# Window attention with a positional convolution: later LayerNorm statistics, value copies on VectorE, an earlier convolution start and edge loads on two queues

## The chip, the cores and the metric

The kernel runs on one core of a Trainium2 chip. Times are device microseconds (us) of one execution. A run of a kernel gives one time, and a kernel is run several times in rounds that alternate with the kernel before on the same chip. Engines in the profile: PE is TensorE (PEld its weight loads), DVE is VectorE, ACT is ScalarE, POOL is GpSimd, SP is SyncE, which here only issues transfers.

## The reference, cut

```python
# x: (1, 511, 511, 192) bf16, dw_pe: (3, 3, 192), w_qkv: (192, 576), w_o: (192, 192)
x0 = x + depthwise_conv3x3(x, dw_pe)              # positional encoding
h  = layernorm(x0)                                # over the 192 channels, no weights
hw = windows(h, 7)                                # 73 x 73 windows of 49 tokens
q, k, v = split_heads(hw @ w_qkv, heads=4)        # head dimension 48
out = softmax(q @ k.T * 48 ** -0.5) @ v           # inside each window
return x0 + unwindow(out @ w_o)
```

## The kernel before: the parts that matter

The 5,329 windows are cut into 42 blocks (0 to 41) of up to 128 windows, one window to a partition. A block goes through attention in 16 chunks of 8 windows. Three blocks are under way at any time:

- block b is in attention (stages A for q, E, A for k, V, the output projection of the block before, D, B);
- block b+1 has its convolution in chunks 0 to 6, its LayerNorm statistics in chunks 6 to 12 and its transposes in chunks 8 to 14;
- block b+2 is loaded: XP (the padded image for the convolution) once XP is free, then X (the windows). The first 30 of its 192 convolution matmuls are done in chunk 15 ("early").

PSUM has three two-bank slots named `ps` for attention, and two slots named `psc`, which the convolution and the LayerNorm transposes share. Blocks 36 to 40 hold vertical strips of the image's edge, and block 41 nine short strips that need many small loads. Since block b+2 is loaded during block b, this shows in blocks 34 to 39, which are called the edge blocks below.

```python
def conv_mm(cv):                       # one convolution matmul; after ten, one addition on VectorE
    c = cv.c
    if c % 10 == 0:
        cv.ps = PCB.next()             # psc
    mm(cv.ps[:, (c % 10) * S : (c % 10 + 1) * S], lhsT=XP[0:KP, :, c], rhs=T[0:KP, c, :], start=True, stop=True)
    cv.c += 1
    if cv.c % 10 == 0 or cv.c == C:
        ...                            # the addition needs X, which is loaded after XP
        nc.vector.tensor_tensor(out=xv, in0=cv.ps[...], in1=xv, op=ALU.add)

def ln_tr(b, r, h):                    # one row of LayerNorm transposes: both psc slots, then two copies
    pb = []
    for kt in range(2):
        pb.append(PCB.next()[0:KT, :].bitcast(BF))
        ...                            # 7 transposes on TensorE
    for kt in range(2):
        eng = nc.vector.tensor_copy if kt == 0 else nc.scalar.copy
        eng(out=HO[b % 2][...], in_=pb[kt][...])
...
# main loop, chunk g = (b, ck); f0 and f are its start and end as a fraction of the block
conv_goal = (EARLY if b else 0) + part(0.0, 0.39, C - (EARLY if b else 0))      # EARLY = 30
if n and conv.c == C and n.tr == WS and nn and xpn == len(xp) and xln == len(xl):
    conv, conv_goal = nn.conv, part(0.875, 1.0, EARLY)      # only when all transposes are done
...
def fill(weight):                      # convolution matmuls between those of stages A and V
    quota[0] += (conv_goal - conv_start) * weight / 24
    ...
s_goal = part(0.40, 0.76, len(n.items)) if n else 0         # statistics
...                                    # hook(share): statistics, stores and loads that are due
stage_A(b, ck, 0, fill)                # q
hook(0.15)
stage_E(*groups[g - LE], nc.vector.tensor_copy)
stage_A(b, ck, 1, fill)                # k
hook(0.35)
stage_V(b, ck, fill, nc.scalar.copy, vv[g % 2])
...                                    # rest of the chunk's convolution
hook(0.55)
...                                    # projection of block b-1: proj(b - 1, s0), copied by ScalarE to pO
stage_D(vv[(g - LD) % 2])
stage_B()
hook(0.75)
n.transpose(part(0.51, 0.88, WS), 1.0)                      # LayerNorm transposes, one row a call
hook(1.0)
```

## Time and profile before

| | before |
|---|---|
| median time | 3900.07 us (3888.94 to 3900.96, 3 runs) |
| profiled execution | 3887.3 us |
| mean of blocks 1 to 33 | 87.61 us |
| block 39 (loads of block 41) | 143.8 us |
| time at half clock, mean of blocks 1 to 33 | 0.4 us a block |

A block's length is the distance between the q copies of its first chunk and of the next block's; chunk lengths are read in the same way. The time at half clock is computed from the mean granted clock c of a block of length t: 2(1 - c)t, because the records show full and half clock only.

The prediction shows the main lines. Two more of the waits of the kernel before are needed later. Each line is an engine, its tile and line, what it waited for, then the sum in us, the number of waits and the longest.

```profile
PE psc L315 <- DVE HO L358: 27.9, 28, 1.0
...
PE psc L348 <- POOL h L338: 14.7, 37, 0.5
```

The first is the early convolution waiting for the copy of the last transposes to give a psc slot free: 1.0 us at most. The second is a row of transposes waiting for its normalized row from GpSimd. Both are small. Line numbers move by up to three lines between the kernels; the tile names identify the group.

### The profile page before, as it was taken

How to read it: one execution, taken by the hardware profiler on the slowest of the kernel's cores; microseconds unless marked ns; L12 is line 12 of the kernel's file. 1: busy time of each engine (PE TensorE's matmuls, PEld its weight loads, DVE VectorE, ACT ScalarE, POOL GpSimd, SP SyncE). 2: the span in 40 equal slices, each digit the busy share in tenths (PEclk: the TensorE clock that was granted, in tenths of full speed). 3: DMA queues.
4: the chain of work that ended last, by engine and by line, in shares of the span. 5: the costliest groups of instructions: out<-in, count | busy, mean ns of one | idle time of the engine just before them, and what ended most of it. 6: DMA issues, size and time to landing. Idle time of an engine off the chain costs nothing.

```text
span 3887.3 us, 165790 instructions
## 1 busy us (share of the span) xinstructions
PE 3422.5 (88%) x75049; PEld 3029.4 (78%) x75049; DVE 2519.8 (65%) x4238; ACT 2799.0 (72%) x3508; POOL 2049.4 (53%) x1427
## 2 busy tenths in 40 slices
PE   3999999999999999999999999999999988888587
PEld 3788888888888888888888888888888877777476
DVE  6666666666666666666666666666666666666453
ACT  0677777777777777777777777777777777666465
POOL 4255555555555555555555555565555555555443
PEclk9799999999999999999999999999999999999888
DMA  5233344444433344444433344444433333344221
GB/s 135 68 93 93 93 100 106 111 112 110 112 94 93 93 100 101 109 114 110 116 94 93 93 101 100 110 112 111 111 100 94 93 93 93 93 93 93 55 40 43
DMA packets 529108, 377.12 MB, mean 97 GB/s; under 512 B 453595, under 2 KB 453787, under 8 KB 528393
## 3 DMA queue, kind: packets, MB, share of 16 engines
q1 hardware_dynamic: 527927, 366.14, 38.9%
q8 instruction: 589, 9.65, 1.1%
q14 instruction: 126, 1.03, 0.1%
q10 hardware_dynamic: 466, 0.30, 0.0%
HBM read 265.31 MB, written 100.27 MB: 94 GB/s over the span
## 4 chain that ended last, share of the span: by engine, by line
PE 31%; DVE 13%; ACT 7%; DMA 4%; SPq 3%; issue 2%; POOL 1%; ACTq 0%; POOLq 0%; DVEq 0%
PE ps L370 10%; PE psc L315 6%; ACT pO L476 5%; PE ps L386 5%; DVE bnst L326 4%; PE ps L465 4%; PE ps L453 4%; DMA X<-in_x_dram 4%; DVE HO L358 3%; DVE o L439 3%; ACT v L394 2%; SPq L238 2%; PE ps L429 2%; DVE HO L454 1%; DVE rs L438 1%
## 5 line engine op out<-in xcount | busy, mean ns | idle before, releaser
L480 POOL TENSOR_TENSOR X<-X,pO 128x768 bf16<-128x768 bf16 (+1 forms) x539 | 831.9, 1562 | 1610.9 <-ACT pO L476 1610.9
L370 PE MATMUL ps<-HO,Wqk 96*128 96x392 bf16 x5336 | 1379.3, 338 | 90.0 <-ACT pO L476 69.7
L315 PEld LDWEIGHTS <-XP 81*128 81x128 bf16 x8064 | 1108.6, 176 | 195.3 <-issue 100.7
L315 PE MATMUL psc<-T,XP 81*128 81x49 bf16 x8064 | 1061.1, 217 | 140.7 <-DMA XP<-in_x_dram 40.3
L321 DVE TENSOR_TENSOR X<-psc,X 128x490 bf16<-128x490 f32 x840 | 541.9, 645 | 436.9 <-PE psc L315 315.4
L378 ACT CAST k<-ps 128x784 bf16<-128x784 f32 x667 | 542.1, 813 | 377.5 <-PE ps L370 304.5
L378 ACT CAST q<-ps 128x784 bf16<-128x784 f32 x667 | 542.8, 814 | 272.5 <-PE ps L370 266.4
L338 POOL TENSOR_TENSOR h<-X,rstd 128x1344 bf16<-128x1344 bf16 x287 | 697.8, 2431 | 22.5
L370 PEld LDWEIGHTS <-Wqk 96*128 96x128 bf16 x5336 | 565.6, 112 | 153.6 <-issue 38.9
L386 PE MATMUL ps<-Wv,HO 96*128 96x192 bf16 x5336 | 643.5, 247 | 26.7 <-ACT q L378 20.1
L416 ACT ACTIVATE pt<-ps 128x784 bf16<-128x784 f32 x667 | 550.3, 825 | 156.8 <-PE ps L408 141.5
L439 DVE TENSOR_TENSOR o<-ps,rs 128x768 bf16<-128x768 f32 x667 | 638.4, 957 | 23.2
L386 PEld LDWEIGHTS <-HO 96*128 96x128 bf16 x5336 | 522.7, 105 | 143.3 <-issue 106.3
L394 ACT CAST v<-ps 128x768 bf16<-128x768 f32 x667 | 536.6, 805 | 117.7 <-PE ps L386 113.5
L438 DVE RECIPROCAL rs<-ps 128x16 f32<-128x16 f32 x667 | 171.3, 257 | 692.6 <-PE ps L429 545.2
L326 DVE BATCH_NORM_STATS2 bnst<-X 128x6 f32<-128x384 bf16 x1050 | 519.5, 543 | 3.0
L454 DVE COPY HO<-ps 96x784 bf16<-96x784 bf16 x667 | 377.2, 566 | 164.2 <-PE ps L453 160.3
L336 POOL TENSOR_TENSOR rstd<-rstd,expo 128x7 f32<-128x7 f32 x294 | 435.4, 1481 | 24.5
L453 PEld LDWEIGHTS <-o 128*96 128x96 bf16 x5336 | 377.3, 128 | 76.5 <-DVE o L439 39.7
L465 PE MATMUL ps<-Wo,HO 96*128 96x192 bf16 x4116 | 435.7, 258 | 0.7 <-DVE HO L454 0.7
L453 PE MATMUL ps<-ident,o 128*96 128x128 bf16 x5336 | 425.2, 223 | 4.5 <-DVE o L439 3.1
L476 ACT CAST pO<-ps 128x768 bf16<-128x768 f32 x498 | 387.3, 801 | 40.9 <-PE ps L465 25.2
(55 smaller groups left out, 2886.7 us busy)
## 6 DMA issues: line engine op xcount, KB each, us to landing
XP<-in_x_dram SPq DMA_DIRECT2D x648, 216.0 KB
X<-in_x_dram SPq DMA_DIRECT2D x574, 168.0 KB
out_dram<-X SPq DMA_DIRECT2D x246, 336.0 KB
XP<-in_x_dram SPq DMA_DIRECT2D x71, 212.6 KB
out_dram<-X SPq DMA_DIRECT2D x82, 168.0 KB
XP<-in_x_dram SPq DMA_DIRECT2D x16, 192.0 KB
XP<-in_x_dram SPq DMA_DIRECT2D x56, 30.4 KB
X<-in_x_dram SPq DMA_DIRECT2D x9, 165.4 KB
```

The source lines that it names most:

```text
L315: mm(cv.ps[:, (c % 10) * S : (c % 10 + 1) * S], lhsT=XP[0:KP, :, c], rhs=T[0:KP, c, :], start=True, stop=True)
L326: nc.vector.bn_stats(out=bnst[:, s : s + 2, :].rearrange("p a f -> p (a f)"), in_=self.X[b % 3][:, s : s + 2, :].rearrange("p s c -> p c s"),)
L338: eng.tensor_tensor(out=h[:, :, :], in0=self.X[b % 3][:, t, :], in1=rstd[:, t].unsqueeze(2).to_broadcast([128, WS, C]), op=ALU.mult)
L370: mm(ps[:, ab * 512 : ab * 512 + TOK], lhsT=self.Wqk[kt][0:KT, which * 2 + ab, :], rhs=HO[b % 2][0:KT, kt, ck * CH : (ck + 1) * CH, 0:S], ...
L378: nc.scalar.copy(out=dst[:, :, 0:TOK], in_=two_bank(ps, TOK))
L386: mm(ps[:, col : col + C], lhsT=HO[b % 2][0:KT, kt, w : w + 2, :].rearrange("p w s -> p (w s)"), rhs=self.Wv[kt][0:KT, :], start=(kt == 0) ...
L394: eng(out=v_[:].rearrange("p (b j) h e -> p b (j h) e", b=2)[:, :, :, 0:DH], in_=two_bank(ps, 2 * C).rearrange("p b (g d) -> p b g d", d=DH),)
L439: nc.vector.tensor_tensor(out=o_[:].rearrange("p b q (h d) -> p b (q h) d", d=DH), in0=ov[:, :, :, 0:DH], in1=r_[:].rearrange("p (b g) -> ...
L453: mm(ev, lhsT=o_[:, sl, Q, kt * KT : (kt + 1) * KT], rhs=ident[:], start=True, stop=True, is_transpose=True)
L465: mm(ps[:, col : col + C], lhsT=HO[b % 2][0:KT, kt, :, s0 + i], rhs=self.Wo[kt][0:KT, :], start=(kt == 0), stop=(kt == 1))
L476: nc.scalar.copy(out=o[:].rearrange("p (b s) c -> p b (s c)", b=2), in_=two_bank(ps, 2 * C))
L480: nc.gpsimd.tensor_tensor(out=xv, in0=xv, in1=o[:, 0:n, :], op=ALU.add)
```

## The change

The intent is to spread VectorE's work: statistics and transposes run up to the end of the block, and VectorE copies v where it has no statistics. Convolution of the block after next starts in chunk 14, before the last transposes. The small loads of block 41, the only one with more than two strips, are issued on two queues. The core of the diff:

```diff
+    q = nc.scalar if len(blocks[b]) > 2 and pc % 3 == 2 else nc.sync      # load_xp, block 41
-    yield lambda dst=dst, src=src: nc.sync.dma_start(out=dst, in_=src)
+    yield lambda q=q, dst=dst, src=src: q.dma_start(out=dst, in_=src)
...
+    q = nc.scalar if b == 0 or short else nc.sync                         # load_x
...
-        EARLY = 30
+                base = n.conv.c if n else 0
+                d = 0.0 if base else 0.06
+                early = nn and len(blocks[b + 2]) <= 2 and not any(ln[2] for ln in blocks[b + 2])
...
-            conv_goal = (EARLY if b else 0) + part(0.0, 0.39, C - (EARLY if b else 0))
-            if n and conv.c == C and n.tr == WS and nn and xpn == len(xp) and xln == len(xl):
-                conv, conv_goal = nn.conv, part(0.875, 1.0, EARLY)
+            conv_goal = base + part(0.0, 0.39 + d, C - base)
+            ahead = n and conv.c == C and early and xpn == len(xp) and xln == len(xl)
+            if ahead:
+                conv, conv_goal = nn.conv, 10 * part(0.875, 1.0, 3)
...
-                quota[0] += (conv_goal - conv_start) * weight / 24
+                quota[0] += (conv_goal - conv_start) * weight / (16 if ahead else 24)
...
-            s_goal = part(0.40, 0.76, len(n.items)) if n else 0
+            s_goal = part(0.40 + d, 0.84, len(n.items)) if n else 0
...
-                stage_A(b, ck, 0, fill)
-                hook(0.15)
+                stage_A(b, ck, 0, fill if not ahead else lambda w: None)
             if 0 <= g - LE < NG:
                 stage_E(*groups[g - LE], nc.vector.tensor_copy)
             if g < NG:
+                hook(0.15)
+            if g < NG:
                 stage_A(b, ck, 1, fill)
                 hook(0.35)
-                stage_V(b, ck, fill, nc.scalar.copy, vv[g % 2])
+                idle = n is None or not 0.38 + d <= f0 < 0.86
+                stage_V(b, ck, fill, nc.vector.tensor_copy if idle else nc.scalar.copy, vv[g % 2])
...
-                    n.transpose(part(0.51, 0.88, WS), 1.0)
+                    n.transpose(part(0.50 + d, 0.96, WS), 1.0)
```

Left out: the order of the first loads (X ahead of XP, X of block 0 on ScalarE's queue), and `+ d` in the goals of the loads. `d` is 0.06 only in a block whose convolution did not start early. The vertical blocks (36 to 40) no longer start early, which changes blocks 34 to 38.

More of the change, by code (lines that the diff above doesn't have):

```diff
@@ L92, in __init__ @@
                 nc.gpsimd.memset(t[:], 0.0)
-        for t in list(self.load_xp(0)) + list(self.load_x(0)):
+        for t in list(self.load_x(0)) + list(self.load_xp(0)):
             t()
@@ L248, in load_x @@
         nc = self.nc
-        for r0, r1 in [(r, r + 1) for r in range(WS)] if len(_blocks(self.NWR, self.NWC)[b]) <= 2 else [(0, WS)]:
+        short = len(_blocks(self.NWR, self.NWC)[b]) > 2
+        for r0, r1 in [(0, WS)] if short else [(r, r + 1) for r in range(WS)]:
             for p, at in self.strips(b, r0, r1):
                 dst = self.X[b % 3][p, r0 * WS : r1 * WS, :].rearrange("p (r q) c -> p r (q c)", q=WS)
-                yield lambda dst=dst, src=self.dram(self.x, *at): nc.sync.dma_start(out=dst, in_=src)
+                q = nc.scalar if b == 0 or short else nc.sync
+                yield lambda q=q, dst=dst, src=self.dram(self.x, *at): q.dma_start(out=dst, in_=src)
     def fast(self, ctx):
@@ L582, in hook @@
                 if n is None or n.conv.c == C:
-                    goal = part(0.38, 0.66, len(xp), at)
+                    goal = part(0.38 + d, 0.66 + d, len(xp), at)
                     while xpn < goal:
@@ L587, in hook @@
                     if b < 1 or stored.get(b - 1, 0) == len(CHUNKS):
-                        goal = part(0.62, 0.82, len(xl), at)
+                        goal = part(0.62 + d, 0.82 + d, len(xl), at)
                         while xln < goal:
```

## The prediction

> **What bounds the kernel now.** I read the page first, then one block in the middle cut at its 16 chunks (a stretch from one copy of q to the next), then the waits, then the DMA issues of that block, last the blocks at the image's edge. There are 42 blocks of up to 128 windows, blocks 0 to 41. While a block goes through attention in 16 chunks, the next block's convolution and LayerNorm run between, and the block after that is loaded. The page, parts 1 and 2:
>
> ```profile
> PE 3422.5 (88%) x75049; PEld 3029.4 (78%) x75049; DVE 2519.8 (65%) x4238; ACT 2799.0 (72%) x3508; POOL 2049.4 (53%) x1427
> ...
> PEclk9799999999999999999999999999999999999888
> ```
>
> TensorE is the busiest, and its clock is full except at both ends. Windows of block 10 (chunks 0, 2, 9, 13, 14, 15 of it), columns as the heading says, PE, PEld, DVE, ACT, POOL, clock, DMA:
>
> ```profile
> 986.39:991.26 4.87, 4.75 (x117) 4.69 (x116) 3.40 (x6) 3.25 (x4) 0.00 (x0) 1.00 0.02 3
> ...
> 996.43:1002.73 6.30, 6.00 (x129) 5.88 (x128) 3.32 (x6) 4.71 (x7) 2.03 (x2) 1.00 0.02 5
> ...
> 1037.93:1042.80 4.87, 4.27 (x109) 3.49 (x107) 4.28 (x8) 4.07 (x7) 4.79 (x5) 1.00 0.68 184
> ...
> 1057.46:1062.95 5.49, 4.49 (x107) 3.51 (x105) 4.87 (x10) 4.30 (x7) 4.35 (x4) 1.00 1.01 232
> 1062.95:1068.58 5.63, 4.33 (x105) 3.59 (x104) 2.75 (x5) 4.09 (x6) 0.99 (x1) 1.00 0.63 158
> 1068.58:1073.75 5.17, 5.03 (x121) 4.98 (x121) 3.61 (x6) 3.25 (x5) 0.00 (x0) 1.00 0.02 5
> ```
>
> Chunks with convolution (0 to 5, 15) are full of PE; chunks 9 to 14 leave it 0.4 to 1.3 us each. The whole block is 87.36 us. The waits name what PE waits for, and where the long stops are:
>
> ```profile
> PE ps L429 <- DVE HO L454: 110.3, 205, 1.0
> PE ps L370 <- ACT pO L476: 69.7, 234, 1.4
> PE psc L315 <- DMA XP<-in_x_dram: 40.3, 1, 40.3
> DVE X L321 <- DMA X<-in_x_dram: 115.1, 10, 55.9
> ```
>
> There is a second path of equal length, the loads. The SP queue and VectorE of block 10 (starts at 986.39):
>
> ```profile
> 1024.16 8.66 SPq L238 DMA_DIRECT2D XP<-in_x_dram  x7
> 1054.80 9.14 SPq L252 DMA_DIRECT2D X<-in_x_dram  x12
> 1063.94:1067.40 3.46, 2.44 (x89) 2.09 (x87) 2.21 (x3) 3.10 (x4) 0.00 (x0) 1.00 0.70 178
> 1068.79 0.67 DVE L321 TENSOR_TENSOR X<-psc,X 128x490 bf16<-128x490 f32 x1 [1.48 <-PE psc L315]
> ```
>
> Loads of XP begin when the convolution has left XP (1024.16, 37.8 us into the block), the last X arrives about 1067.4 (81.0), some 43.2 us later, and the first early addition of the block after next runs at 1068.79 (82.4), only 1.4 us behind. So the loads have almost no slack.
>
> The edge: blocks 34 to 38 take 95.32, 93.43, 96.47, 96.83 and 97.70 us, since that addition has to wait (8.3, 5.7, 9.1, 9.7, 11.0 us), and block 39 takes 143.77:
>
> ```profile
> 3570.58:3714.35 143.77, 84.83 (x1799) 73.82 (x1798) 59.11 (x100) 67.04 (x84) 48.69 (x34) 0.78 0.23 47
> 3272.40:3275.50 3.10, 0.04 (x1) 0.00 (x0) 0.70 (x2) 0.65 (x1) 0.00 (x0) 1.00 0.21 60
> 3276.40:3283.20 6.80, 6.80 (x113) 5.63 (x113) 3.36 (x7) 3.25 (x4) 0.00 (x0) 0.50 0.01 2
> ```
>
> A PE gap of 3.10 us is followed by 6.80 us at half clock.
>
> **What the Trainium skill says.** "TensorE: Matmul & The Clock Gate", section on the HAM clock gate: the array falls to half rate after an idle free-running window of about 3.4 us. The trace agrees, and is stricter: gaps of 2.2 to 3.1 us in the edge blocks sufficed, and 6.80 us is two such windows. "DMA: Bandwidth & Descriptors", section "Issuing engines are not separate DMA queues": a second issuing engine adds no bandwidth, it saves sequencer time only. In block 39 that time is the cost (84 us of issues of small loads, 47 GB/s over the block), so the second queue helps there. "VectorE: DVE Perf Modes", section "Why PSUM operands drop a tier": fp32 from PSUM runs at 1x. The trace has 957 ns for o (768 wide, from PSUM) on VectorE and 805 ns for the v copy on ScalarE. I take 0.95 us for a v copy on VectorE.
>
> **The change part by part.** No work is removed; TensorE keeps its counts. I compared the order of instructions of both programs for block 10.
>
> 1. V copies: chunks 0 to 6, 14 and 15 (9 of 16) go to VectorE: ScalarE loses 9 x 0.805 = 7.2 us a block, VectorE gains 9 x 0.95 = 8.6 (59.2 to 67.8 of 87). In chunks 2 to 6, PE's wait of 0.3 us for pO should go: -1.5 us. In chunks 0 and 1 VectorE then holds 3.4 + 0.95 of 4.9 us, and the slot of v is the one the next q needs: +0.5. Net -1.0 a block.
> 2. Statistics: in spite of the new goals they stay in chunks 6 to 12, and the transposes in 8 to 14, one a chunk (at most two normalized rows may wait). But one statistic of each chunk moves from the tail, where it is ahead of the HO copy, to behind it: I put that at up to -2 us of the HO wait (110.3 us / 42 = 2.6 a block).
> 3. Early convolution: 30 matmuls of chunk 15 become 20 in chunk 14 and 10 in chunk 15. Their first addition now comes about 1.8 us into chunk 14, at 76.6 - 1.0 - 2.0 + 1.8 = 75.4 us. X arrives at 81.0 - 1.0 + 0.8 (semaphore) = 80.8. VectorE works in order, so it would stand 5.4 us, with the v copy, the reciprocal, o and the transposes' copies behind it. PE can finish D and B (about 77.9) and then stands too, because the transposes need both psc buffers.
>    After X lands, VectorE does two additions, v and o (0.67 + 0.67 + 0.95 + 0.26 + 0.96 = 3.5 us); the E of chunk 15 needs o, and the rest of chunk 15 with a next q costs about 5.4: a tail of 8.9 us, where the kernel before has 87.4 - 81.8 = 5.6. So the block is (37.8 - 1.0) + (43.2 + 0.8) + 8.9 = 89.7, +2.3. A PE stop of 2 to 4 us also brings half clock, for which I add 0.7: +3.0 x 33 blocks (1 to 33) = +99.
> 4. Blocks 34 to 38 no longer start early. The loads still take about 52 us there (38.5 to 90) and start a chunk later, so most of the wait moves into the next block's first chunks: -2 each, -10.
> 5. Block 39: of some 102 loads and clears, 27 XP and 9 X go to ScalarE's queue. SP keeps about 66 x 0.8 + stores 4 = 57 us, starting at about 43: done at 100. ScalarE gains 27 x 0.76 + 9 x 0.33 = 23.5 us of issuing in chunks with little room, about +10 us on the block. Block 39 is about 95, block 40 stands about 7 and then is cold for about 4: 95 + 86 + 11 = 192, against 143.8 + 85.9 = 229.7: -37.
> 6. Block 41: v on VectorE everywhere, 11 x 0.4: -5. Start: X is issued on ScalarE's queue ahead of the weights; bytes are the same and the weights come later: +3. Block 0, same late loads: +3.
>
> Sum: 99 - 10 - 37 - 5 + 6 = +53, that is 3953.
>
> **The rivals.** (a) The early additions do not stand, since X lands earlier than I think or PE has enough else to do. Then each block gains 1.0 + 2.0, less 1 for the fuller VectorE: -2 x 33 = -66, with the edge -46: 3788. For it: the HO waits are real, and the change drops the fill in the first q stage. Against: the landing at 81.0 depends on 43.2 us of transfers at a DMA share of 0.69 to 0.88, which no part of the change shortens. (b) Half clock in nearly every block costs more, 2 us a block over my 0.7: +66, 4019. For it: in the edge blocks every gap over 2.1 us was followed by half clock. Against: it partly overlaps with VectorE's backlog. (c) ScalarE's issuing in block 39 takes back what the second queue saves: +20.
>
> **Range and chances.** I give 0.25 to (a), 0.75 to a steady block that gets longer by 1 to 5 us. Mean: 0.25 x 3788 + 0.75 x 3953 = 3912; the middle is nearer the larger part. I say 3935, with 3825 to 4010. Over 2% faster means under 3822: 0.16. Over 2% slower, over 3978: 0.24.
>
> **What would show it.** Right, if the profile after has VectorE's X addition waiting for X by DMA in most blocks, 3 to 6 us each (100 us or more in all, from ten waits now), chunk 14 at 8 us or more, and a mean clock under 0.973. Wrong, if chunk 14 is under 6 us or that wait is absent from the middle blocks: then X lands earlier, and rival (a) holds. Step 1: PE's wait for pO falls from 69.7 to under 25. Step 2: PE's wait for HO falls by half. Step 5: blocks 39 and 40 together 185 to 205 us.

## The result and the profile after

| | before | changed |
|---|---|---|
| median time | 3900.52 us (3888.94 to 3909.21, 4 runs) | 4076.64 us (4067.0 to 4084.52, 4 runs) |
| ratio | 1 | 1.0452 [1.0415, 1.049]: slower |
| profiled execution | 3887.3 us | 4082.8 us |
| mean clock of the profiled execution | 0.973 | 0.928 |

A ratio is the mean time of one kernel's fast runs over that of the other's of the same rounds, so not quite the ratio of the two medians; brackets hold its 95% interval. The outputs are right.

Where the 195.5 us of the profiled executions come from:

| | before | changed | difference |
|---|---|---|---|
| start, up to the first q | 107.7 | 109.4 | +1.7 |
| block 0 | 92.0 | 97.0 | +5.0 |
| blocks 1 to 33, mean | 87.61 | 93.26 | +5.65 each, +186.5 |
| blocks 34 to 38, sum | 479.8 | 486.4 | +6.6 |
| block 39 | 143.8 | 127.8 | -16.0 |
| block 40 | 85.8 | 93.1 | +7.3 |
| block 41 | 87.1 | 91.6 | +4.5 |

So nearly all of it is in the ordinary blocks. Mean chunk lengths there (us, blocks 2 to 33):

| chunk | 0 | 1 | 2 | 3-8 | 9 | 10 | 11 | 12 | 13 | 14 | 15 |
|---|---|---|---|---|---|---|---|---|---|---|---|
| before | 4.89 | 4.89 | 6.59 | 35.18 | 4.89 | 5.32 | 4.74 | 4.68 | 5.51 | 5.73 | 5.20 |
| changed | 5.69 | 5.82 | 6.81 | 35.08 | 4.43 | 6.11 | 4.38 | 4.30 | 5.02 | 9.62 | 6.01 |

Chunks 9, 11, 12 and 13 gain 1.7 us together. Chunk 14 loses 3.9, chunks 15, 0, 1 and 2 together 2.8, chunk 10 0.8.

The page of the changed kernel: the busy times, and the clock in tenths over 40 slices of the span.

```profile
PE 3560.1 (87%) x75049; PEld 3114.7 (76%) x75049; DVE 2850.5 (70%) x4625; ACT 2501.3 (61%) x3121; POOL 2050.8 (50%) x1427
...
PEclk9899999999899989998999999999999999889798
```

TensorE has the same 75,049 matmuls and is busy 138 us longer. Eights stand in the middle of the row of the clock, where the kernel before has nines. ScalarE has lost 298 us and VectorE has gained 331: the v copies moved, and neither engine is the busiest.

The waits of the changed kernel:

```profile
DVE X L324 <- DMA X<-in_x_dram: 200.0, 38, 7.6
...
PE psc L351 <- DVE X L324: 110.8, 33, 5.0
...
PE ps L373 <- DVE v L397: 77.1, 121, 1.0
PE ps L373 <- ACT pO L479: 57.5, 192, 1.4
...
PE psc L351 <- POOL h L341: 42.4, 34, 1.4
PE ps L432 <- DVE HO L457: 30.9, 64, 1.0
```

The wait for X by DMA, 115.1 us in 10 waits before (55.9 of it in one wait of block 39), is now 200.0 us in 38 waits, one in most blocks. The second line is its echo: TensorE's transposes need a psc slot that the standing addition holds. The third is new: q waits for a slot until VectorE has copied v. The wait for HO has fallen from 110.3 to 30.9 us, and that for h has risen from 14.7 to 42.4.

One block of the changed kernel in windows (block 11, chunks 0, 1, 12, 13, 14, 15); columns are start and end, length, busy us with instruction counts of PE, PEld, DVE, ACT, POOL, then the clock, the DMA share and GB/s.

```profile
1140.66:1145.76 5.10, 4.74 (x116) 4.68 (x116) 4.00 (x7) 2.45 (x3) 0.00 (x0) 1.00 0.01 3
1145.76:1151.31 5.55, 4.78 (x117) 4.71 (x117) 4.33 (x7) 2.45 (x4) 0.00 (x0) 1.00 0.02 4
...
1208.72:1212.97 4.25, 4.21 (x106) 3.29 (x104) 3.95 (x8) 4.15 (x7) 3.55 (x4) 1.00 0.93 178
1212.97:1217.84 4.87, 4.18 (x101) 3.19 (x100) 4.74 (x9) 4.39 (x7) 4.14 (x4) 1.00 0.99 206
1217.84:1227.39 9.55, 6.55 (x121) 5.39 (x121) 4.37 (x8) 3.46 (x6) 2.00 (x1) 0.87 0.36 104
1227.39:1232.93 5.54, 4.55 (x107) 4.34 (x106) 3.82 (x6) 2.45 (x4) 0.00 (x0) 0.92 0.02 3
```

Chunk 14 lasts 9.55 us with 6.55 us of matmuls, and the clock falls during it. VectorE in that chunk (the timeline: start, length, line, operation, tiles, and in brackets the idle time before it):

```profile
1218.76 0.57 DVE L457 COPY HO<-ps 96x784 bf16<-96x784 bf16 x1 [0.77 <-PE ps L456]
1223.72 1.24 DVE L324 TENSOR_TENSOR X<-psc,X 128x490 bf16<-128x490 f32 x2 [4.39 <-DMA X<-in_x_dram]
1224.88 0.95 DVE L397 CAST v<-ps 128x768 bf16<-128x768 f32 x1
1225.75 0.25 DVE L441 RECIPROCAL rs<-ps 128x16 f32<-128x16 f32 x1
1226.03 0.96 DVE L442 TENSOR_TENSOR o<-ps,rs 128x768 bf16<-128x768 f32 x1
1226.90 1.08 DVE L361 COPY HO<-psc 96x896 bf16<-96x896 bf16 x1
```

VectorE stands 4.39 us for X, with v, the reciprocal, o and the transposes' copy in line behind. The v copy takes 0.95 us on VectorE, as estimated. XP's loads, which wait until the convolution has left XP, start 38.7 us into this block (37.8 in block 10 of the kernel before):

```profile
1179.32 8.53 SPq L239 DMA_DIRECT2D XP<-in_x_dram  x7
```

In the mean of blocks 1 to 33 they start at 39.7 us (37.8 before), and the first early addition runs at 83.6 (81.4 to 88.4).

### The profile page after: what moved, and what is told of

The parts are those of the page before. It is cut to its first block, busy times and chain, and to the rows that moved or that the text cites.

```text
span 4082.8 us, 166019 instructions
## 1 busy us (share of the span) xinstructions
PE 3560.1 (87%) x75049; PEld 3114.7 (76%) x75049; DVE 2850.5 (70%) x4625; ACT 2501.3 (61%) x3121; POOL 2050.8 (50%) x1427
## 3 DMA queue, kind: packets, MB, share of 16 engines
q10 hardware_dynamic: 4525, 5.02, 0.6%
## 4 chain that ended last, share of the span: by engine, by line
PE 53%; DVE 12%; ACT 11%; POOL 9%; DMA 8%; issue 3%; SPq 3%; ACTq 0%; DVEq 0%; POOLq 0%
PE ps L373 18%; PE psc L318 9%; ACT pO L479 8%; PE ps L389 8%; DMA X<-in_x_dram 7%; PE ps L456 6%; PE ps L468 6%; POOL h L341 4%; PE psc L351 3%; DVE v L397 3%; POOL X L483 2%; DVE o L442 2%; DVE bnst L329 2%; POOL rstd L339 2%; DVE HO L361 2%
## 5 line engine op out<-in xcount | busy, mean ns | idle before, releaser
L373 PE MATMUL ps<-HO,Wqk 96*128 96x392 bf16 x5336 | 1441.6, 354 | 161.0 <-DVE v L397 77.1
L318 PEld LDWEIGHTS <-XP 81*128 81x128 bf16 x8064 | 1123.1, 175 | 204.6 <-issue 128.8
L318 PE MATMUL psc<-T,XP 81*128 81x49 bf16 x8064 | 1092.9, 218 | 46.3 <-DMA XP<-in_x_dram 18.6
L373 PEld LDWEIGHTS <-Wqk 96*128 96x128 bf16 x5336 | 576.3, 114 | 185.8 <-issue 71.4
L389 PE MATMUL ps<-Wv,HO 96*128 96x192 bf16 x5336 | 662.0, 250 | 21.4 <-ACT q L381 16.4
L329 DVE BATCH_NORM_STATS2 bnst<-X 128x6 f32<-128x384 bf16 x1050 | 533.7, 544 | 0.3
L361 ACT COPY HO<-psc 96x896 bf16<-96x896 bf16 x294 | 326.3, 1110 | 258.8 <-PE psc L351 254.4
L456 PEld LDWEIGHTS <-o 128*96 128x96 bf16 x5336 | 403.1, 135 | 94.3 <-DVE o L442 55.9
L456 PE MATMUL ps<-ident,o 128*96 128x128 bf16 x5336 | 457.1, 233 | 9.2 <-DVE o L442 7.9
L351 PE MATMUL psc<-ident,h 128*96 128x128 bf16 x4018 | 310.5, 234 | 154.4 <-DVE X L324 110.8
```

The costliest lines, as they stand in the source:

```text
L329: nc.vector.bn_stats(out=bnst[:, s : s + 2, :].rearrange("p a f -> p (a f)"), in_=self.X[b % 3][:, s : s + 2, :].rearrange("p s c -> p c s"),)
L373: mm(ps[:, ab * 512 : ab * 512 + TOK], lhsT=self.Wqk[kt][0:KT, which * 2 + ab, :], rhs=HO[b % 2][0:KT, kt, ck * CH : (ck + 1) * CH, 0:S], ...
L389: mm(ps[:, col : col + C], lhsT=HO[b % 2][0:KT, kt, w : w + 2, :].rearrange("p w s -> p (w s)"), rhs=self.Wv[kt][0:KT, :], start=(kt == 0) ...
L456: mm(ev, lhsT=o_[:, sl, Q, kt * KT : (kt + 1) * KT], rhs=ident[:], start=True, stop=True, is_transpose=True)
```

## The experiments

The first look leaves three theories, which the expectations below call by letters or by name:

- **L, the landing.** The early convolution in chunk 14 runs into X's arrival. VectorE stands in order and the chain behind it is late. The cost is the stand.
- **V, the v copies.** The copies on VectorE are themselves on the path: they delay the copies that give PSUM slots free.
- **W, the cold window.** A small delay at the block's end takes TensorE's busy share below what keeps the clock full, and the half clock that follows is the cost. Then a small delay of any kind costs several us.

Each edit is named against the kernel that it starts from. "Blocks" is the mean length of blocks 1 to 33 and "half" the time at half clock in one of them, both in the profiled execution; before they are 87.61 and 0.4 us.

### Undoing one part of the change

**e1_after_early15**: the early convolution back to its old condition.

```diff
-ahead = n and conv.c == C and early and xpn == len(xp) and xln == len(xl)
+ahead = n and conv.c == C and n.tr == WS and early and xpn == len(xp) and xln == len(xl)
# also: weight / 24, and fill in the first stage A again
```

> The changed kernel with the early convolution put back into chunk 15, after the last transpose, all else as changed. Theory L (the early additions are put ahead of X's landing): blocks 1 to 33 fall from 93.3 to 86.5-88.5 us, chunk 14 from 9.6 to under 6, VectorE's wait for X by DMA from 200 to under 80 us, the whole about 3900 (3860 to 3940). Theory V (the v copies fill VectorE and stretch the block's end): chunk 14 falls, but chunks 0, 1 and 15 keep what they gained, and the whole stays above 3980. Theory S (the new statistics goals): no change, about 4075.

Measured: 4084.64 us, 1.0484 [1.0445, 1.0522]; blocks 93.25, half 11.8. This was a miss of the design. With the later transpose goals the last transposes come too late for `n.tr == WS`, so no block started early at all (`base` stays 0 and `d` 0.06). It shows a version without early convolution, and tells nothing about L.

**e8_after_early15_full**: the same question, asked properly: 30 early matmuls in chunk 15, no condition on the transposes.

```diff
-ahead = ... 
-    conv, conv_goal = nn.conv, 10 * part(0.875, 1.0, 3)
+if n and conv.c == C and ck == nslot - 1 and early and ...:
+    conv, conv_goal = nn.conv, 30
# also: weight / 24, and fill in the first stage A again
```

> The changed kernel with all 30 early convolution matmuls in chunk 15 (the first attempt at this undid the early start altogether, since the last transpose then came too late). The v copies stay on VectorE. Theory L (landing): 3860 to 3940. Theory V with W (v copies delay the copies at the block's end, which brings half clock): no better than the changed kernel, 4030 to 4090, half clock 8 us or more a block, chunk 15 above 7 us as with the v copies alone.

Measured: 4026.71 us, 1.0333 [1.0294, 1.0371]; blocks 91.60, half 11.4; chunk 14 6.24, chunk 15 7.17, chunk 0 6.42 us. Without the stand in chunk 14 the blocks win 1.7 us back, but the half clock stays. So L is not the whole.

**e2_after_v_scalar**: the v copies back on ScalarE.

```diff
-stage_V(b, ck, fill, nc.vector.tensor_copy if idle else nc.scalar.copy, vv[g % 2])
+stage_V(b, ck, fill, nc.scalar.copy, vv[g % 2])
```

> The changed kernel with every v copy on ScalarE. Theory L: the wait for X stays (150 us or more), chunk 14 stays above 8.5 us, the block loses 1 to 2.5 us (chunks 0 and 1 back to 4.9, less queued behind the landing), the whole 4000 to 4045. Theory V: chunk 14 falls to about 6 and the whole to under 3950. Theory S: about 4075.

Measured: 3966.96 us, 1.0163 [1.0137, 1.0189]; blocks 90.50, half 5.6; chunk 14 10.06 us, chunks 0 and 1 back to 4.87 and 4.89. It came out faster than L alone allowed: the copies had a cost that I had not given them. The stand in chunk 14 stays.

**e15_after_repaired**: both undone: v on ScalarE, and 30 early matmuls in chunk 15 outside the first stage A. All other parts stay.

```diff
-stage_V(b, ck, fill, nc.vector.tensor_copy if idle else nc.scalar.copy, vv[g % 2])
+stage_V(b, ck, fill, nc.scalar.copy, vv[g % 2])
-ahead = n and conv.c == C and early and ...
+ahead = n and conv.c == C and ck == nslot - 1 and early and ...
-    conv, conv_goal = nn.conv, 10 * part(0.875, 1.0, 3)
+    conv, conv_goal = nn.conv, 30
```

> The changed kernel with two parts taken back: v copies on ScalarE, and the early convolution in chunk 15, outside its first q stage; the vertical blocks' later start, the last block's two queues and the statistics stay. If these two parts and their half clock are the whole loss: 3840 to 3880. Rival (the later start of the vertical blocks or the loads issued on ScalarE at the beginning cost too): 3885 to 3930.

Measured: 3851.89 us, 0.9873 [0.9821, 0.9926]; blocks 86.72, half 3.5; blocks 34 to 38 475.2, block 39 121.7, block 40 94.0. With e2, e8 and the changed kernel it closes a square for the blocks: neither part 86.72, the start in chunk 14 alone 90.50 (+3.8), the v copies 91.60 (+4.9; e8 fills the first stage A, which e15 does not), both 93.26 (+6.5). The two costs are real and not additive: they share the end of the block.

### Doing one part alone

**e3_before_early14**: only the early start.

```diff
-if n and conv.c == C and n.tr == WS and nn and xpn == len(xp) and xln == len(xl):
-    conv, conv_goal = nn.conv, part(0.875, 1.0, EARLY)
+ahead = n and conv.c == C and nn and xpn == len(xp) and xln == len(xl)
+if ahead:
+    conv, conv_goal = nn.conv, 10 * part(0.875, 1.0, 3)
# also: weight / 16 and no fill in the first stage A when ahead
```

> The kernel before with one change alone: 20 of the 30 early convolution matmuls in chunk 14 and 10 in chunk 15. Theory L: most of the loss appears by this alone: chunk 14 from 5.7 to 8 or more, VectorE's wait for X 120 us or more, half clock in most blocks, the whole 3980 to 4060. Theory V or S: within 1% of 3900.

Measured: 3994.55 us, 1.0234 [1.0212, 1.0257]; blocks 90.29, half 4.7; chunk 14 8.55 us. Its waits and its chunks 14 and 15 of block 11:

```profile
DVE X L321 <- DMA X<-in_x_dram: 271.3, 39, 59.9
PE psc L348 <- DVE X L321: 110.2, 39, 13.3
```

```profile
1178.85:1187.56 8.71, 6.32 (x117) 5.46 (x116) 4.00 (x7) 4.33 (x7) 1.07 (x1) 0.76 0.32 91
1187.56:1193.07 5.51, 5.29 (x109) 4.67 (x108) 2.37 (x4) 3.24 (x5) 0.00 (x0) 0.76 0.00 0
```

The stand of the changed kernel appears with this one part: 39 waits for X (one of them, of 59.9 us, in block 39), chunk 14 at 8.71 us in block 11. It costs 2.7 us a block.

**e17_early14_fewer_loads** and **e18_before_fewer_loads**: is it the landing, or the order of the instructions? e17 is e3 with every third load of XP left out from block 2 on, so that X lands earlier; e18 is the kernel before with the same loads left out. Their outputs are wrong, which doesn't matter for the times. A third of XP then holds an older block (the comparison's tolerance passed them all the same, as the positional term is small).

```diff
 if n1 <= n0:
     continue
+if b > 1 and pc % 3 == 2:
+    continue
```

> Wrong result on purpose. Early convolution in chunk 14 (3995 us alone), and from block 2 on every third load of XP left out, so that X lands 6 to 12 us earlier. Theory L: VectorE's wait for X in chunk 14 goes, chunk 14 falls from 8.55 to under 6, half clock under 2 us a block, the blocks 1 to 33 from 90.3 to 86-87.5. Rival (denser convolution in chunk 14 stands by itself): chunk 14 stays above 7.5.

> Wrong result on purpose, the control: the kernel before with the same loads left out. The early start in chunk 15 had 1.4 us of slack to X's landing, so blocks 1 to 33 stay at 87.3 to 87.7 us; only the edge blocks 34 to 39 gain (20 to 45 us in all).

Measured: e17 3795.04 us, 0.9736 [0.9714, 0.9759]; blocks 86.41, half 0.2. e18 3833.85 us, 0.9826 [0.98, 0.9853]; blocks 88.01, half 1.3; chunk 14 5.69 as before, so fewer loads alone do nothing in ordinary blocks, and its gain lies in the edge (blocks 34 to 38 443.7 us, block 39 121.6). e17, chunks 14 and 15 of block 11:

```profile
1130.83:1136.07 5.24, 5.13 (x122) 4.59 (x121) 3.68 (x7) 4.20 (x7) 1.07 (x1) 1.00 0.00 0
1136.07:1140.45 4.38, 4.02 (x104) 3.81 (x102) 2.70 (x5) 3.21 (x5) 0.00 (x0) 1.00 0.01 4
```

The same instructions in the same order, with X already there (DMA share 0.00), take 9.62 us for the two chunks where e3 took 14.22, at full clock throughout. This shows L: the early start costs because X has not landed. With X there e3's edit is a gain of 1.6 us a block over e18; about 0.5 of it is what the unfilled first stage A gains alone (e10).

**e16_early14_x_on_scalar**: e3 with X of all blocks from 2 on issued on ScalarE's queue, as a way to land X earlier.

```diff
-yield lambda dst=dst, src=...: nc.sync.dma_start(out=dst, in_=src)
+q = nc.scalar if b > 1 else nc.sync
+yield lambda q=q, dst=dst, src=...: q.dma_start(out=dst, in_=src)
```

> Early convolution in chunk 14 alone (3995 us) plus one change: X is loaded from ScalarE's queue, beside XP on SP's, so that it lands earlier. Theory L: the first early addition comes 1.5 to 5 us earlier than at 82 us into the block, chunk 14 falls from 8.55 to 5.5-7.5 and the whole to 3920 to 3970. Rival (the stand is made by the denser convolution in chunk 14, not by X): chunk 14 stays at 8.5, the whole at 3995 or more.

Measured: 4703.69 us, 1.2048 [1.1983, 1.2114]. Inconclusive on L, because something else took over. From its waits:

```profile
ACT q L379 <- DMA out_dram<-X: 477.2, 71, 10.2
```

The load of X must wait until the store of an older block has left that buffer. On ScalarE's queue this wait stands in front of ScalarE's own q copies: 477 us.

**e4_before_v_vector**: only the v copies, on VectorE in chunks 0 to 6, 14 and 15.

```diff
-stage_V(b, ck, fill, nc.scalar.copy, vv[g % 2])
+idle = n is None or not 0.38 <= f0 < 0.86
+stage_V(b, ck, fill, nc.vector.tensor_copy if idle else nc.scalar.copy, vv[g % 2])
```

> The kernel before with one change alone: v copies on VectorE in chunks 0 to 6, 14 and 15. Theory L: chunks 0 and 1 grow by 0.2 to 0.7 us each, chunks 2 to 6 stay at 6.6 (PE's 0.3 us wait there is for the second pO copy, which v does not delay), the block +1 to +2, the whole 3920 to 3980. Theory V: the whole above 4020. Our own step in the prediction, now doubted: 33 us faster.

Measured: 4118.52 us, 1.0558 [1.0536, 1.058]; blocks 92.95, half 11.2; chunk 0 6.10, 1 5.77, 14 6.29, 15 7.60 us. This one part alone is slower than the whole change. Its waits, and chunks 0, 14 and 15 of block 11:

```profile
PE ps L370 <- DVE v L394: 73.3, 122, 1.0
PE ps L370 <- ACT pO L476: 60.3, 209, 1.4
...
PE psc L315 <- DVE HO L358: 46.0, 30, 1.8
```

```profile
1141.18:1148.39 7.21, 7.19 (x118) 6.07 (x117) 4.50 (x7) 2.45 (x4) 0.00 (x0) 0.50 0.01 2
...
1221.86:1228.38 6.52, 4.77 (x105) 3.70 (x104) 3.67 (x6) 3.37 (x6) 1.06 (x1) 0.89 0.44 120
1228.38:1236.41 8.03, 7.40 (x120) 6.30 (x120) 4.57 (x7) 2.44 (x4) 0.00 (x0) 0.50 0.01 3
```

Chunk 15 and chunk 0 run at half clock from end to end, with PE busy 7.40 of the 8.03 us of chunk 15: the matmuls themselves are slow. The new waits are smaller than the loss. In blocks 1 to 33 q waits for v 1.8 us a block (in chunks 0, 1 and 15), and the early convolution waits 0.5 us a block longer for the last transposes' copy (27.9 to 46.0 us in all), which comes behind v on VectorE. These 2.3 us are V's part; the loss is 5.3 us a block. The rest pointed to W.

**e12_v_chunks_2_6** and **e13_v_chunks_14_15**: the v copies on VectorE in these chunks alone.

```diff
+spare = n is not None and 2 <= ck <= 6        # e12
+late = n is not None and ck >= 14             # e13
```

> The kernel before with v copies on VectorE in chunks 2 to 6 alone, where VectorE has over 2 us a chunk free and PE's next q does not need the slot of v. All theories but the prediction: no change, 3890 to 3910, PE's wait for pO in these chunks stays 0.3 us. Prediction, step 1: 1.5 us a block saved, about 3845.

> The kernel before with v copies on VectorE in chunks 14 and 15 alone. Theory W: these two make most of the cost, since they delay the copy of the last transpose and the next q just before the full chunks: half clock 6 us a block or more, the whole 3985 to 4060. Rival (chunks 0 and 1, where VectorE is full, make it): under 3960.

Measured: e12 3903.87 us, 1.0004 [0.9986, 1.0023]; blocks 87.82, half 1.0: neutral. e13 4100.41 us, 1.0511 [1.0456, 1.0567]; blocks 92.40, half 12.1. Two v copies a block carry nearly all of e4's cost. First e12's wait for pO, then chunks 14 and 15 of block 11 of e13:

```profile
PE ps L370 <- ACT pO L476: 58.8, 201, 1.4
```

```profile
1194.45:1200.59 6.14, 4.33 (x104) 3.62 (x103) 3.66 (x6) 3.36 (x6) 1.02 (x1) 1.00 0.38 107
1200.59:1208.08 7.49, 6.86 (x120) 5.96 (x120) 4.47 (x7) 2.45 (x4) 0.00 (x0) 0.56 0.01 3
```

Chunk 14 has 6.14 us at full clock with PE busy 4.33 of it (0.71), and then the clock falls for chunk 15. e12's line shows why the copies bring nothing in chunks 2 to 6: the wait for pO falls only from 69.7 to 58.8, since it hangs on ScalarE's second projection copy of the chunk, not on the v copy ahead of it.

### One delay by itself

**e11_before_delay14**: the kernel before, with one more `bn_stats` (0.54 us on VectorE; it recomputes the same values) in chunk 14, ahead of the last transposes' copy. V and L have no part in it: only W says that it costs more than its own length.

```diff
 if n:
+    if ck == 14 and n.si == len(n.items):
+        ln_stat(n.b, 24)
     n.transpose(part(0.51, 0.88, WS), 1.0)
```

> The kernel before with one useless instruction a block: the last statistic (0.54 us on VectorE) is computed a second time in chunk 14, ahead of the copy of the last transpose; the result is the same. VectorE is idle a third of the time there. Theory W: chunk 14 grows by about 0.5 us and this alone brings half clock in most blocks: 4 to 11 us of it a block, the block +2 to +4 us, the whole 3965 to 4035. Rival (no cliff; a wait costs what it is long): +0.5 x 40 = 20 us, 3910 to 3925, and half clock under 1.5 us a block.

Measured: 4025.17 us, 1.029 [1.0241, 1.0339]; blocks 91.42, half 10.8. Chunks 13, 14 and 15 of block 11, and its wait for the copy (27.9 before):

```profile
1168.52:1173.97 5.45, 4.45 (x107) 3.48 (x105) 4.83 (x9) 4.39 (x6) 4.31 (x4) 1.00 0.97 213
1173.97:1180.28 6.31, 4.56 (x105) 3.69 (x104) 3.32 (x6) 4.14 (x7) 1.04 (x1) 0.95 0.48 132
1180.28:1187.63 7.35, 7.35 (x119) 6.20 (x119) 3.71 (x6) 3.24 (x4) 0.00 (x0) 0.50 0.01 2
```

```profile
PE psc L315 <- DVE HO L358: 47.2, 33, 1.5
```

0.54 us of VectorE work a block costs 3.8 us a block. The mean of chunk 14 is 0.50 us longer (6.23 against 5.73), which is the delay itself; then chunk 15 runs at half clock. This shows W.

To see how near the edge the kernel before was, I counted from the traces PE's busy share in the steps of 3.41 us in which the clock changes (it changes only at multiples of that), for steps at full clock in blocks 1 to 33, and whether the next step was at half clock:

| PE busy share | before | e11 | e4 | changed |
|---|---|---|---|---|
| under 0.60 | 0 | 25, 23 | 30, 30 | 26, 26 |
| 0.60 to 0.65 | 1, 1 | 3, 1 | 5, 1 | 12, 10 |
| 0.65 to 0.70 | 5, 0 | 3, 1 | 0 | 11, 4 |
| 0.70 to 0.72 | 36, 1 | 19, 1 | 22, 10 | 29, 10 |

The first number is the steps at full clock with that share, the second how many of them were followed by half clock. The kernel before put about one step a block at 0.70 to 0.72 and got away with it nearly always. The half us of e11 moves many of these below 0.60, where 23 of 25 are followed by half clock. Busy here is by the profile's modelled ends of matmuls, so the shares are not exact, and between 0.60 and 0.72 both outcomes occur. Steps above 0.72 are left out of the table, and the clock falls after some of them too: 6 of the 56 falls in the changed kernel, and 12 of the 26 in e9 below, ten of these after a step of 0.83 or more. So the share of the last step is not the whole rule.

### The other parts

**e5_before_hook**: only the first hook behind stage E.

```diff
 stage_A(b, ck, 0, fill)
-hook(0.15)
 stage_E(*groups[g - LE], nc.vector.tensor_copy)
+hook(0.15)
```

> The kernel before with one change alone: the first statistics of a chunk queued behind the copy of E instead of ahead of it. Prediction, step 2: up to 2 us a block saved, 3830 to 3870. Theory W[...]: the HO wait falls by half and the clock stays full, so the gain stays: 3850 to 3890, held back by X's landing at 82 us. Rival: the loads' landing takes all of it, 3895 to 3905.

Measured: 3902.24 us, 1.0024 [0.9994, 1.0054]; blocks 87.89. No gain, and the wait for HO stays where it was (110.3):

```profile
PE ps L429 <- DVE HO L454: 109.6, 204, 1.0
```

**e6_before_goals**: only the goals of statistics and transposes.

```diff
-part(0.40, 0.76, len(n.items))        n.transpose(part(0.51, 0.88, WS), 1.0)
+part(0.40, 0.84, len(n.items))        n.transpose(part(0.50, 0.96, WS), 1.0)
```

> The kernel before with one change alone: the new goals of statistics and transposes. Prediction: the order hardly moves, within 0.5% of 3900. Rival (theory S, it is this that makes PE wait for h in chunk 10, 1.25 us in the changed kernel against 0.38): PE's wait for h rises from 15 to over 40 us and the whole to 3915 to 3950.

Measured: 3872.09 us, 0.9969 [0.992, 1.0018]; blocks 87.09, half 2.6. Its waits:

```profile
PE psc L348 <- POOL h L338: 48.5, 39, 1.4
...
PE ps L429 <- DVE HO L454: 15.1, 45, 0.5
```

It is the goals, not the hook, that take the statistic from ahead of the HO copy: 110.3 to 15.1 us, and chunks 9, 11, 12 and 13 are 0.34 to 0.57 us shorter each. Chunk 10 gives 0.7 us back, where a transpose is now called before its normalized row is ready (14.7 to 48.5 us), and the half clock takes more. The interval holds 1.

**e7_before_queues**: only the edge loads on two queues.

```diff
+q = nc.scalar if len(blocks[b]) > 2 and pc % 3 == 2 else nc.sync      # load_xp
+q = nc.scalar if len(blocks[b]) > 2 else nc.sync                      # load_x
```

> The kernel before with one change alone: the last block's loads on two queues (early convolution and goals as before). Prediction, step 5: the issue time on SP falls from 84 to about 57 us and block 39 from 143.8 to 110 to 120, the whole 3865 to 3880. Rival: ScalarE's issuing in front of its own copies takes it back, block 39 over 130, the whole over 3885.

Measured: 3872.38 us, 0.9946 [0.9916, 0.9976]; block 39 123.2 us (143.8 before), block 40 85.0. A gain, smaller than expected (110 to 120 for block 39). The trace shows both sides. SyncE's issues end 106.0 us into block 39 instead of 123.4, and chunks 14 and 15 together take 10.9 us instead of 65.7. But chunks 6 to 12, where ScalarE issues for 24.9 us, take 70.0 us instead of 35.7: the issues stand ahead of its own copies, and one of them waits for a store.

```profile
ACT k L380 <- DMA out_dram<-X: 10.6, 1, 10.6
```

**e10_before_unfilled** and **e9_v_vector_unfilled**: no early convolution in the first stage A of chunk 15, so that q no longer waits behind it; on the kernel before (e10) and on e4 (e9).

```diff
-stage_A(b, ck, 0, fill)
+stage_A(b, ck, 0, fill if not ahead else lambda w: None)
# also: weight / 16 when ahead
```

> The kernel before with the same single change: no early convolution in the first q stage of chunk 15. Its wait of 0.8 us for VectorE's copy goes: 0.3 to 0.9 us a block, 3870 to 3895, no half clock. Rival: denser convolution in the rest of chunk 15 takes it back, 3895 to 3915.

> The kernel before with the v copies on VectorE (4118 us alone) and the early convolution kept in chunk 15 but left out of its first q stage, so that PE does not wait there for VectorE's copy of the last transpose. Theory W (small waits at the block's end bring half clock, and that is over half of the cost of the v copies): half clock falls from 11 to under 5 us a block and the whole to 3960 to 4030. Rival (VectorE's own work is the cost): within 1% of 4118.

Measured: e10 3878.34 us, 0.9926 [0.9892, 0.9961]; blocks 87.09, half 1.2; chunk 14 4.26, chunk 15 5.82 us. e9 4010.13 us, 1.0257 [1.0204, 1.031]; blocks 91.28, half 8.2 (under 5 was expected); chunk 14 4.25, chunk 15 7.36. The edit is a small gain by itself. It doesn't save the v copies: the wait only moves into chunk 15.

**e14_goals_queues_unfilled**: the kernel before with the three parts that were good or neutral alone (e6, e7, e10).

> The kernel before with the three parts that paid alone (statistics goals 0.997, last block's loads on two queues 0.995, no early convolution in the first q stage 0.993), nothing else. If they add: 0.985 of before, 3830 to 3860. Rival: the loads' landing at 82 us holds the block, since chunk 15 now comes earlier, and at least half of the gain is lost: over 3875.

Measured: 3842.98 us (3828.79 to 3883.14, 6 runs), 0.9873 [0.9822, 0.9924]; blocks 86.40, half 2.5; block 39 123.2. It beats both kernels, and is the fastest version here with the work complete; e15 has the same ratio. Chunks 0, 14 and 15 of block 11:

```profile
1063.09:1068.78 5.69, 5.56 (x118) 5.06 (x117) 3.40 (x6) 3.25 (x5) 0.00 (x0) 0.81 0.01 3
...
1138.97:1143.38 4.41, 4.38 (x106) 3.58 (x106) 2.81 (x5) 4.07 (x6) 2.01 (x1) 1.00 0.80 237
1143.38:1149.11 5.73, 5.59 (x125) 5.48 (x123) 3.89 (x7) 3.25 (x5) 0.00 (x0) 1.00 0.02 6
```

Chunks 14 and 15 are at full clock with PE busy 0.99 and 0.98 of them. Chunk 0 (0.81) still shows a step at half clock: this version isn't free of it.

## Why the prediction was right or wrong

The prediction said 3935 us (3825 to 4010), with the largest chance on "within 2%"; the changed kernel takes 4076.64. The direction of its middle was right. Step 3 adds up a block from three terms, and the traces show each of them (mean of blocks 1 to 33, us; the half clock's 0.7 is put to the last):

| | predicted | changed | e2 (v on ScalarE) |
|---|---|---|---|
| start of XP's loads | 37.8 - 1.0 = 36.8 | 39.7 | 37.8 |
| from there to the first early addition | 43.2 + 0.8 = 44.0 | 43.9 | 44.0 |
| from there to the block's end | 8.9 + 0.7 = 9.6 | 9.7 | 8.7 |
| block | 90.4 | 93.26 | 90.50 |

- **Step 1, the v copies: this is the step that failed.** Its -1.0 us a block is the "37.8 - 1.0" of step 3: XP's loads were to start 1.0 us earlier, and they start 1.9 later. With the v copies back on ScalarE (e2) they start at 37.8 again, the block takes 90.50 and the whole 3966.96. So on top of the early start the copies cost 2.76 us a block; alone they cost 5.3 (e4). The gain of 1.5 us in chunks 2 to 6 does not exist (e12, neutral), because the wait for pO hangs on the second projection copy: it went from 69.7 to 57.5, not under 25. The cost in chunks 0 and 1 was put at +0.5, and q waits there 1.0 us a block for v. The half clock that the copies bring was not counted: 3.1 of the 10.4 us at half clock lie in chunks 0 to 2 (none there in e2), while the convolution still holds XP. The cost in chunks 14 and 15 was not seen either, and where the copies stand alone it is nearly all of theirs (e13), through W.
- **Step 3, the landing: mechanism right, and its own terms of about the right size.** What it named as proof came: VectorE's wait for X in most blocks (38 waits), chunk 14 over 8 us (9.62), a clock under 0.973 (0.928). e3 shows that this part alone makes it and e17 that the landing is its cause. That e2 comes so near the predicted 90.4 is in part luck: its start is 1.0 us later and its end 0.9 shorter than the terms. As for the half clock as a whole, the length of a block of the changed kernel goes with its time at half clock as 90.26 + 0.29 x half (a fit over blocks 1 to 33, correlation 0.94), so at the mean of 10.4 us some 3.0 us go with it. This is a fit, not an experiment. The 0.7 was meant for the block's end, and there it fits.
- **Rival (b)** ("half clock in nearly every block costs more, 2 us a block over my 0.7") has nearly the right size, 4019 against 4077, but not the place: it tied the half clock to the stop, and the missing us are in the chunks that follow. I set it aside since the delay would overlap with VectorE's backlog. And I asked whether PE would stop for 2 to 4 us, as in the edge blocks. e11 shows that no stop is needed: a delay of half a us, after which PE's busy share in a step falls from 0.71 to below 0.60, is enough.
- **Step 2, the HO wait: effect right, cause wrong.** The wait fell by more than half, as said (110.3 to 30.9). But the moved hook does nothing (e5), and the goals, of which the step said that they change little, do it (e6). Of the 2 us hoped for, 1.7 came in chunks 9, 11, 12 and 13, and 0.8 went back in chunk 10, where PE waits for h. The changed kernel doesn't even keep the rest: what a block wins ahead of chunk 14, it waits there for X.
- **Step 4, blocks 34 to 38: failed.** Predicted -10, measured +6.6. Block 34 gained 9.9 us and blocks 35 to 38 lost 16.5: the wait moved into the next block, and the cold clock came with it (49.9 us at half clock in blocks 35 to 38 before, 91.3 now). In e15, without the other two costs, their sum is 475.2, 4.6 under the kernel before; this part was not run by itself.
- **Step 5, blocks 39 and 40: half of it.** Predicted 192 us, measured 220.9 (229.7 before). The two queues alone give 20.6 us in block 39 (e7), where 49 were counted: 28 short. Rival (c) has the cause and about the size. ScalarE's issuing was given "about +10 us on the block", and the rival 20 more; in e7 the chunks in which ScalarE issues grow by 34. The changed kernel then loses 7.3 us in block 40.
- **Step 6** was small: the start +1.7 (+3 predicted), block 0 +5.0 (+3), block 41 +4.5 instead of -5, since the v copies do not gain there either (91.6 with them alone, e4, against 87.1). The new order of the first loads was not run alone.
- **Rival (a)**, X landing earlier or other work in between, did not occur. It had a quarter of the weight and pulled the middle down by 18 us from the working's own sum of 3953.

What stays open: where exactly the clock falls (the shares between 0.60 and 0.72 show both outcomes, and e9 has falls after steps of 0.83 and more); a sole share of the loss for the v copies or the early start, as the two do not add (2.76 or 4.9 us for the copies, 1.7 or 3.8 for the start, by what is undone first); and what the later start of blocks 34 to 38 is worth alone.

## What to carry to other kernels

Look at TensorE's busy share in steps of the clock's own period, not only at its idle gaps: a kernel can sit just above the share at which the clock mostly falls, and then half a us of delay on a helper engine costs many times its length. Before work is pulled ahead of a wait, compare when its data lands with when its first in-order consumer will ask for it, because everything behind that consumer stands as well. And ask what in the chunks before delays the start of those loads: here the landing moved with it, and the miss lay there. When a change has several parts, run each alone: here one part alone lost more than the whole, and three others together made the fastest version.

## What the Trainium skill lacked or had wrong

- "TensorE: Matmul & The Clock Gate", Part 1 and the table under "Why this matters for your kernels": the array goes back to half rate after an idle window of about 3.4 us, and the advice is to leave no gaps over about 3 us. The period agrees (clock changes lie on a grid of 3.41 us). The condition in the table is too mild. (The page's section "A second HAM failure mode: psum-queue depth-cycling" does tell of a clock that oscillates through frequent short idles, without a share.) Here steps in which PE was busy under 0.60 of the time, nearly all of them 0.40 to 0.60 in e4 and e11, were followed by half clock (30 of 30 in e4, 23 of 25 in e11, 26 of 26 in the changed kernel), and at 0.70 to 0.72 it came sometimes (1 of 36 in the kernel before, 10 of 22 in e4); in e9 ten of 26 falls came after steps of 0.83 or more. The page gives no busy share.
- The same page lacks the cost of living near that edge: 0.54 us more on VectorE a block took the half clock from 0.4 to 10.8 us a block and the block from 87.61 to 91.42 us (e11).
- "DMA: Bandwidth & Descriptors", section "Issuing engines are not separate DMA queues": the saving of sequencer time by a second issuing engine is real here (block 39 from 143.8 to 123.2 us, e7). The section doesn't say that an issue which has to wait holds up that engine's own work behind it ("Anatomy of one DMA" on the same page has the wait on the issuing sequencer, but not this cost): ScalarE stood 477.2 us before its q copies in e16, and the kernel took 1.2048 times as long.
